# Shorter pauses between indirect transfers in a planned order, and a plan whose durations are read from a trace

## The chip, the cores and the metric

One core of a Trainium2 chip runs the whole kernel. The metric is the device time of one execution in microseconds, as the median of several runs. Five engines work beside each other, each on its own list of instructions in a fixed order: PE (matmuls), DVE (vector), ACT (activations and copies), POOL (here above all the issue of indirect transfers, and sums), and SP (the issue of plain transfers). Semaphores tie them together.

## What is computed

Pooled attention makes x, and a mixture of experts that takes the best expert for each token makes the output:

```python
q_pool = q.reshape(B, H, S // 2, 2, D).mean(axis=3)          # B=8, H=8, S=1152, D=64
scores = np.matmul(q_pool, k.transpose(0, 1, 3, 2)) / np.sqrt(D)
attn = softmax(scores)                                        # over the 1152 keys
x = np.matmul(attn, v).transpose(0, 2, 1, 3).reshape(4608, 512)

logits = x @ w_gate                                           # 8 experts
expert_idx = np.argmax(logits, axis=1)
for e in range(8):                                            # w1[e]: 512x1024, w2[e]: 1024x512
    xe = x[expert_idx == e]
    out[expert_idx == e] = gate_w[..., None] * (np.maximum(xe @ w1[e], 0) @ w2[e])
```

## The kernel before

**Attention** runs over 32 pairs (batch, two heads) and in each over two halves of the queries. A half has nine score products on PE (L543), each of which DVE takes out of PSUM (L548, `take`), an exponential on ACT in three pieces (L576), row sums folded on POOL (L622) and summed on PE (L631), and nine products with the values (L647). When the four pairs of a batch are done, the routing finds each token's expert, SP stores the rows of x to a table in DRAM (`x_runs`, L815), and POOL scatters each token's number and weight into its expert's list (`enlist`, L823, six indirect transfers per batch).

**The experts' stage** takes tokens in tiles. Two early tiles of 384 tokens, of the two experts with the most tokens so far, are cut while the last batch still runs. Then come the ranks: eight experts in the order of what is left to them, with tiles of (384, 288), (384, 256), (384, 224), (384, 192), (384, 160), (224, 192), (352) and (160) tokens. For a ranked tile POOL loads its piece of the list (`li`, L908), makes row numbers (`ix`, L918) and the tokens' numbers for the way back (`rec`, L921), and gathers 32 tokens at a time from `x_runs` (L924, `gather`): 12 gathers for 384 tokens. Buffers are `xr` (7) for the first and third 128 tokens of a tile and `xq` (4) for the second. DVE multiplies the rows with the token's weight (L1081, L1082, `weigh`) and transposes them (L1085); ACT casts them to the upper part `xh` (L1089), DVE makes the lower part `xl` (L1044). All products are made of such parts in three matmuls. PE makes the hidden layer (`ph`, L1138, 96 matmuls for a tile), ACT and DVE take it out (`hh` L1145, `hl` L1147), PE makes the output (`py`, L1167, 24 matmuls for every 128 tokens), ACT copies it (`y`, L1185, three buffers), and POOL scatters it to its tokens' places (L1175, `scatter`). The weights come by SP into six raw buffers and are split by ACT (`w1h`, `w2h`, L1106) and DVE (`w1l`, `w2l`, L1044); each part has one buffer, so that an expert's weights can be split only when the products of the one before have read theirs.

**The order** of all five engines is planned in the program, by `Flow`. Every step is added with its engine, a duration in ns, a key (its due place), what it waits for and the buffers that it holds. `emit` runs a model of the chip with these durations and gives each engine its list: whenever an engine is free in the model, it takes the ready step with the lowest key. Steps with the mark `paced` are the indirect transfers of POOL (L823, L924, L1175). Between the end of one in the model and the start of the next, CALM ns must pass. And the pause is made to hold on the chip too: when `trace` writes the instructions out, every paced transfer is tied by `in_step` to the last PE instruction written before it,

```python
if s[12] and self.pe is not None:
    self.pace(made, self.pe)      # a semaphore: no sooner than its place in the order
```

so that POOL, which could issue it when its data are there, waits until PE has ended that instruction. POOL works in order, and whatever stands behind the transfer on POOL waits too. The durations in the calls of `add` have no other use than this plan: no instruction depends on them except by its place.

## Time and profile before

| what | value |
|---|---|
| median of 3 runs | 1315.97 us (1315.13 to 1318.11) |
| profiled execution | 1319.63 us |
| its span | 1318.1 us |
| mean granted TensorE clock | 0.958 of full speed |
| PE busy | 1191.4 us, 90% |
| POOL busy | 878.7 us, 67% |
| DVE busy | 768.3 us, 58% |
| ACT busy | 628.4 us, 48% |

Busy shares are means over two stages: attention, up to about 745 us, and the experts' stage behind it. So the profile is read by stretches first, then by what PE waited for, and then along the engines that it waited for. The times in the rows are of the profiled execution and count from the start of its span. Idle time before an instruction is given with its releaser, the last thing that it waited for as far as semaphores show; "issue" means that nothing of that sort is seen.

### The profile page before, as it was taken

To read this page: it belongs to the slowest core of one execution; us is meant where nothing else is said; L and a number is where in the kernel's file an instruction comes from. 1 tells how busy PE (TensorE), PEld (TensorE's weight loads), DVE (VectorE), ACT (ScalarE), POOL (GpSimd) and SP (SyncE) were. 2 spreads that over 40 slices of the span, in tenths; PEclk is the share of its full clock that TensorE was granted. 3 is DMA by queue.
4 is the path that set the end of the run, shared out by engine and by line. 5 is a ranking of instruction groups with operands and counts; after the bars stand their busy time and mean duration, and the time that the engine had idled before them with its cause. 6 is when DMAs were issued, how large, how long until landed. Compare 5 with 4: busy or idle time off the path is not lost. (4 is left out here: it accounts for less than half of the span.)

```text
span 1318.1 us, 33770 instructions
## 1 busy us (share of the span) xinstructions
PE 1191.4 (90%) x14157; PEld 829.4 (63%) x14157; DVE 768.3 (58%) x2080; ACT 628.4 (48%) x768; POOL 878.7 (67%) x539
## 2 busy tenths in 40 slices
PE   7999999999999999999999897398996969699695
PEld 3555555555555555555555596297886868698695
DVE  5677768768677677687686584324443434334540
ACT  4657566565666666666664543212332222223340
POOL 2999899998999999999962523635454544434430
PEclk9999999999999999999999898799997979799898
DMA  6643334144243442352423256313323332324420
GB/s 181 151 122 86 108 98 145 48 110 130 73 113 106 112 115 82 104 140 63 115 64 115 87 143 187 102 29 99 108 88 110 94 113 75 120 67 139 157 76 19
DMA packets 76082, 138.12 MB, mean 105 GB/s; under 512 B 9859, under 2 KB 33311, under 8 KB 75920
## 3 DMA queue, kind: packets, MB, share of 16 engines
q1 hardware_dynamic: 65088, 116.18, 30.7%
q0 software_dynamic: 9744, 19.64, 5.3%
q8 instruction: 114, 1.87, 0.7%
q14 instruction: 48, 0.39, 0.1%
q10 hardware_dynamic: 1088, 0.03, 0.1%
HBM read 115.04 MB, written 21.02 MB: 103 GB/s over the span
## 5 line engine op out<-in xcount | busy, mean ns | idle before, releaser
L548 DVE TENSOR_SCALAR_CACHE_REDUCE s<-st 128x576 f32<-128x576 f32 x576 | 417.2, 753 | 166.9 <-PE st L543 166.0
L576 ACT ACTIVATE s<-s,bias 128x1728 f32<-128x1728 f32 x192 | 321.0, 1730 | 174.7 <-DVE bias L572 174.3
L543 PE MATMUL st<-qT,kT 64*64 64x288 f32 x4608 | 360.0, 411 | 18.6 <-DVE s L548 13.8
L647 PE MATMUL pa<-s,vn 64*64 64x288 f32 x4608 | 346.1, 405 | 0.2
L543 PEld LDWEIGHTS st<-qT,kT 64*64 64x64 f32 x4608 | 159.1, 133 | 164.5 <-DVE s L548 83.3
L622 POOL TENSOR_TENSOR fold<-s 128x1728 f32<-128x1728 f32 x58 | 224.3, 3868 | 14.4 <-ACT s L576 14.2
L1138 PE MATMUL ph<-xh,w1h 128*128 128x384 f32 (+6 forms) x512 | 165.6, 323 | 69.3 <-ACT xh L1089 68.3
L647 PEld LDWEIGHTS pa<-s,vn 64*64 64x64 f32 x4608 | 167.0, 133 | 93.3 <-DVE xT L653 6.7
L622 POOL TENSOR_TENSOR fold<-fold,s 128x1728 f32<-128x1728 f32 x58 | 224.5, 3871 | 1.0
L924 POOL DMA_INDIRECT xr<-x_runs,ix x104 | 118.1, 1136 | 131.6 <-PE ph L1138 43.6
L1138 PE MATMUL ph<-xl,w1h 128*128 128x384 f32 (+6 forms) x512 | 165.1, 322 | 1.0 <-DVE xl L1044 0.8
L1138 PE MATMUL ph<-xh,w1l 128*128 128x384 f32 (+6 forms) x512 | 163.6, 320 | 0.0
L1147 DVE SCALAR_TENSOR_TENSOR hl<-ph,hh 128x384 fp32r<-128x384 f32 (+5 forms) x100 | 55.0, 550 | 165.7 <-ACT hh L1145 154.1
L1138 PEld LDWEIGHTS ph<-xh,w1h 128*128 128x128 f32 x512 | 103.2, 202 | 73.7 <-ACT xh L1089 70.9
L1167 PE MATMUL py<-w2h,hh 128*128 128x512 f32 x328 | 128.7, 392 | 4.3 <-ACT y L1185 4.3
L1167 PE MATMUL py<-w2l,hh 128*128 128x512 f32 x328 | 128.5, 392 | 0.0
L1167 PE MATMUL py<-w2h,hl 128*128 128x512 f32 x328 | 128.3, 391 | 0.0
L1145 ACT ACTIVATE hh<-ph 128x384 fp32r<-128x384 f32 (+5 forms) x100 | 48.5, 487 | 159.6 <-PE ph L1138 157.8
L1175 POOL DMA_INDIRECT out_dram<-y,rec x41 | 44.8, 1092 | 113.0 <-issue 56.3
L1138 PEld LDWEIGHTS ph<-xl,w1h 128*128 128x128 f32 x512 | 102.8, 201 | 4.0 <-DVE xl L1044 3.5
L1138 PEld LDWEIGHTS ph<-xh,w1l 128*128 128x128 f32 x512 | 103.0, 201 | 0.0
L924 POOL DMA_INDIRECT xq<-x_runs,ix x44 | 52.7, 1197 | 62.0 <-PE py L1167 42.4
(176 smaller groups left out, 1313.5 us busy)
## 6 DMA issues: line engine op xcount, KB each, us to landing
raw<-in_moe_w_dram SPq DMA_DIRECT2D x80, 512.0 KB
qn<-in_q_dram SPq DMA_DIRECT2D x64, 384.0 KB
kn<-in_k_dram SPq DMA_DIRECT2D x32, 576.0 KB
vn<-in_v_dram SPq DMA_DIRECT2D x32, 576.0 KB
x_runs<-row SPq DMA_DIRECT2D x24, 396.0 KB
xr<-x_runs,ix POOLq DMA_INDIRECT x104
x_runs<-empty SPq DMA_DIRECT2D x4, 297.0 KB
lists<-re,di POOLq DMA_INDIRECT x48
```

What stands on the lines that cost most here:

```text
L543: made = nc.tensor.matmul(pt.t[to, h, :HQ], x.kT.t[up, c * P + i * D:c * P + (i + 1) * D], x.qT.t[up, cols], start=True, stop=True, tile_p ...
L548: nc.vector.tensor_scalar(s.t[:, c], pt.t[:, :, :HQ], -SCALE, None, op0=ALU.mult, op1=ALU.min, accum_out=mx.t[:, c:c + 1],)
L576: nc.scalar.activation(s.t[:, c0:c0 + n], s.t[:, c0:c0 + n], AF.Exp, bias=bias.t, scale=-1.0)
L622: add = lambda to, a, b: nc.gpsimd.tensor_tensor(to, a, b, ALU.add)
L647: made = nc.tensor.matmul(pa.t[cs, i, :HQ], x.vn.t[up, h, c, :], s.t[up, c, h], start=c == 0, stop=c == NC - 1, tile_position=(up.start, c ...
L924: return nc.gpsimd.indirect_dma_start(out=x.xr[i // NQD].t[:, i % NQD, :], out_offset=None, in_=xg, in_offset=bass.IndirectOffsetOnAxis(ap ...
L1138: made = nc.tensor.matmul(view()[:, i, :], a[:, c, fp], b[:, c, :n], start=c == 0 and k == 0, stop=c == NDC - 1 and k == 2)
L1145: a = f.add("ACT", act(nb * n) - 44, lambda fs=fs, view=view: nc.scalar.activation(hidden(m)[0][:, fs, :n], view(), AF.Relu), at - 20, don ...
L1147: d = f.add("DVE", dve(nb * n), lambda fs=fs, view=view: nc.vector.scalar_tensor_tensor(hidden(m)[1][:, fs, :n], view(), 0.0, hidden(m)[0] ...
L1167: made = nc.tensor.matmul(py.t, a[:, c, hs], b[:, c % 2, :], start=c == 0 and k == 0, stop=c == NFC - 1 and k == 2)
L1175: ins = nc.gpsimd.indirect_dma_start(out=out, out_offset=bass.IndirectOffsetOnAxis(ap=x.re.t[:up, r:r + 1], axis=0), in_=y.t[:up], in_offs ...
```

## The change

The pause gets two values, CALM 700 ns for the scatters into the lists and the gathers of early tiles, and CALM_X 500 ns for the gathers of ranked tiles and the scatters of outputs; `paced` is now that number. Beside this, durations in the plan are replaced: ACT's and POOL's base cost, the reductions, the exponential, PE's products and others. The core of the diff:

```diff
-CALM = 1300
+CALM, CALM_X = 700, 500
...
                 if s[12]:
-                    calm = free[e] + CALM
+                    calm = free[e] + s[12]
...
     def act(n):
-        return 110 + 0.833 * n
+        return 95 + 0.833 * n
...
     def pool(n):
-        return 185 + 2.137 * n
+        return 138 + 2.137 * n
...
-            m = f.add("PE", 460, product, at, done(*x.q[half], *x.k.get(c, ())), [pt, s, x.kT, x.qT], QUADS)
-            taken.append(f.add("DVE", 150 + dve(2 * HQ), take, at, done(m), [pt, s]))
+            m = f.add("PE", 452, product, at, done(*x.q[half], *x.k.get(c, ())), [pt, s, x.kT, x.qT], QUADS)
+            taken.append(f.add("DVE", dve(2 * HQ) + 20, take, at, done(m), [pt, s]))
...
-            e = f.add("ACT", act(2 * n * HQ) + 190, lambda c0=c0, n=n: expo(c0, n),
+            e = f.add("ACT", act(2 * n * HQ) + 95, lambda c0=c0, n=n: expo(c0, n),
...
-            outs.append(f.carry("POOL", 1230, lambda j=j: enlist(j), at + (K_PUT if b is None or b < B - 2 else 0) * j / NJ, done(p, *hold), [di, re], 40, paced=True))
+            outs.append(f.carry("POOL", 1230, lambda j=j: enlist(j), at + (K_PUT if b is None or b < B - 2 else 0) * j / NJ, done(p, *hold), [di, re], 40, paced=CALM))
...
-        x.rows = done(*(f.carry("POOL", 1310, lambda i=i: gather(i), key + i * 3 / x.nb, done(p, *stored), [x.ix, x.xr[i // NQD]], 400, paced=True)
+        x.rows = done(*(f.carry("POOL", 1310, lambda i=i: gather(i), key + i * 3 / x.nb, done(p, *stored), [x.ix, x.xr[i // NQD]], 400, paced=CALM if early else CALM_X)
...
-            p = f.add("DVE", dve(k * P) + 90, weigh, key + r, x.rows[r * NQD:r * NQD + k], [x.xr[r], x.li])
+            p = f.add("DVE", dve(k * P) + 180, weigh, key + r, x.rows[r * NQD:r * NQD + k], [x.xr[r], x.li])
...
-                    p = f.add("PE", 6 * n / 2.4 + 13, product, at,
+                    p = f.add("PE", 6 * max(n / 2.4 + 13, 110), product, at,
...
-                p = f.add("PE", 6 * DM / 2.4 + 14, product, at + c0, done(p, *x.w2_ready[c0 // 2], *x.made.get(c0, ()), *x.made.get(c0 + 1, ())),
+                p = f.add("PE", 6 * (DM / 2.4 + 13), product, at + c0, done(p, *x.w2_ready[c0 // 2], *x.made.get(c0, ()), *x.made.get(c0 + 1, ())),
...
-            a = f.add("ACT", act(DM) + 50, lambda y=y, py=py, up=up: nc.scalar.copy(y.t[:up], py.t[:up]),
+            a = f.add("ACT", act(DM) - 40, lambda y=y, py=py, up=up: nc.scalar.copy(y.t[:up], py.t[:up]),
                       at, done(p), [py, y])
-            f.carry("POOL", 1300, scatter, at, done(a), [y, x.re], 1200, paced=True)
+            f.carry("POOL", 1300, scatter, at, done(a), [y, x.re], 1200, paced=CALM_X)
```

Two places of the order. The first is POOL's list behind the last batch's scatters into the lists, where the first ranked tile is prepared. Before, with the second and the third scatter (L1175) of the first early tile's output, the loads of lists (li_10610 is that of the first ranked tile), its row numbers (ix_10693) and its first gather:

```order
L1175 DMA out_dram<-y_10511,rec_0_9583 4608x512
L884 TENSOR_LOAD ranked
L908 ISA
L908 DMA li_10653<-lists 128x1x18
L1175 DMA out_dram<-y_10569,rec_0_9583 4608x512
L918 TENSOR_SCALAR ix_10693<-li_10610,gid 128x12
L921 COPY rec_2_10695<-li_10610 32x3 x4
L884 TENSOR_LOAD ranked
L908 ISA
L908 DMA li_10710<-lists 128x1x24
L924 DMA xr_10721<-x_runs,ix_10693 128x132
```

After, from the load of the third ranked tile's list on (that of the first and second stand ahead of it; ix_10601 is now the first ranked tile's):

```order
L908 DMA li_10583<-lists 128x1x24
L918 TENSOR_SCALAR ix_10601<-li_10523,gid 128x12
L921 COPY rec_2_10603<-li_10523 32x3 x4
L884 TENSOR_LOAD ranked
L908 ISA
L908 DMA li_10618<-lists 128x1x16
L1175 DMA out_dram<-y_10621,rec_0_9635 4608x512
L918 TENSOR_SCALAR ix_10651<-li_10564,gid 128x9
L921 COPY rec_3_10653<-li_10564 32x3
L921 COPY rec_3_10653<-li_10564 32x2 x3
L924 DMA xr_10670<-x_runs,ix_10601 128x132
```

Two more loads of lists and the first ranked tile's row numbers have moved in front of the third scatter, and one load from behind its row numbers; the second tile's row numbers stand ahead of the first gather now.

The second place is POOL's list at the last gathers of the first tile of the third rank, of 384 tokens, the one whose first product is at 1000.43 in the trace. Its row numbers are ix_10860 before and ix_10801 after, and the outputs y_11796, y_11829, y_11869 before and y_11867, y_11906, y_11942 after are those of the first tile of the second rank. Before:

```order
L924 DMA xq_11965<-x_runs,ix_10860 128x132 x4
L924 DMA xr_12079<-x_runs,ix_10860 128x132 x4
L1175 DMA out_dram<-y_11796,rec_4_10790 4608x512
L1175 DMA out_dram<-y_11829,rec_4_10790 4608x512
L1175 DMA out_dram<-y_11869,rec_4_10790 4608x512
L1175 DMA out_dram<-y_12153,rec_5_10830 4608x512
L924 DMA xr_12196<-x_runs,ix_10883 128x132
```

After:

```order
L924 DMA xq_11735<-x_runs,ix_10801 128x132 x2
L924 DMA xr_11808<-x_runs,ix_10801 128x132 x4
L1175 DMA out_dram<-y_11867,rec_4_10687 4608x512
L924 DMA xr_11884<-x_runs,ix_10834 128x132 x2
L1175 DMA out_dram<-y_11906,rec_4_10687 4608x512
L924 DMA xr_11884<-x_runs,ix_10834 128x132 x2
L1175 DMA out_dram<-y_11942,rec_4_10687 4608x512
L924 DMA xq_11973<-x_runs,ix_10834 128x132 x3
```

Before, all three scatters of the earlier tile, and one of the tile behind it (y_12153), stand behind the last of the twelve gathers. After, the last gathers still stand ahead of these scatters, but the gathers of the next tile (ix_10834) are between the scatters too. A list of one engine does not show which PE instruction each transfer is tied to.

## Rows read from the trace of the kernel before

**Rows 1.** This is the table of stretches (from:to in us from the span's start). Columns: length of the stretch, then for each engine its busy time and in brackets its instructions, then TensorE's granted clock (1.00 is full speed), the DMA engines' mean busy share and GB/s:

```profile
25.00:385.00 360.00, 350.01 (x5753) 197.92 (x5746) 256.76 (x772) 231.30 (x244) 337.94 (x132) 1.00 0.39 106
385.00:745.00 360.00, 350.39 (x5706) 198.80 (x5701) 258.04 (x807) 215.40 (x239) 298.51 (x132) 1.00 0.35 99
...
1050.00:1100.00 50.00, 39.07 (x183) 34.95 (x182) 18.30 (x30) 12.09 (x20) 21.48 (x24) 0.86 0.32 103
...
1150.00:1200.00 50.00, 50.00 (x304) 45.28 (x304) 21.20 (x33) 16.68 (x26) 20.84 (x17) 1.00 0.35 106
```

**Rows 2.** This is the list of waits of PE between 740 and 1318 us. Columns: who waited for whom, then us in total, times, and the longest:

```profile
PE ph L1138 <- ACT xh L1089: 68.3, 7, 22.4
PE m L1026 <- DVE f L1025: 8.7, 1, 8.7
PE py L1167 <- ACT y L1185: 4.3, 1, 4.3
```

**Rows 3.** This is the timeline of PE, the rows that follow an idle time at the start of a tile's first product. Columns: start in us, us, engine, line, operation, out<-in, shape, and in brackets the idle time before it and what ended it:

```profile
856.99 0.69 PE L1138 MATMUL ph<-xh,w1h 128*128 128x384 f32 x1 [22.44 <-ACT xh L1089]
...
930.28 0.44 PE L1138 MATMUL ph<-xh,w1h 128*128 128x384 f32 x1 [1.66 <-ACT xh L1089]
...
1000.43 0.69 PE L1138 MATMUL ph<-xh,w1h 128*128 128x384 f32 x1 [11.00 <-ACT xh L1089]
...
1069.33 0.69 PE L1138 MATMUL ph<-xh,w1h 128*128 128x384 f32 x1 [10.89 <-ACT xh L1089]
...
1136.92 0.69 PE L1138 MATMUL ph<-xh,w1h 128*128 128x384 f32 x1 [9.91 <-ACT xh L1089]
...
1248.74 0.66 PE L1138 MATMUL ph<-xh,w1h 128*128 128x352 f32 x1 [10.61 <-ACT xh L1089]
```

**Rows 4.** This is the table of stretches again, with PE's half-clock stretches and one at full clock:

```profile
856.99:863.30 6.31, 6.27 (x18) 5.87 (x19) 1.23 (x2) 0.49 (x1) 1.06 (x1) 0.50 0.15 48
863.30:876.90 13.60, 13.60 (x80) 13.60 (x80) 4.09 (x8) 2.95 (x6) 6.17 (x10) 1.00 0.09 22
993.04:1006.70 13.66, 6.23 (x18) 5.84 (x19) 3.12 (x6) 2.07 (x4) 3.60 (x4) 0.50 0.40 144
1061.30:1074.96 13.66, 5.59 (x16) 5.19 (x17) 3.71 (x7) 2.02 (x4) 4.28 (x4) 0.50 0.45 164
1129.57:1143.20 13.63, 6.24 (x18) 5.84 (x19) 4.39 (x7) 2.16 (x4) 4.33 (x4) 0.50 0.58 183
1242.20:1252.45 10.25, 3.71 (x12) 3.40 (x13) 3.96 (x7) 1.61 (x3) 2.89 (x4) 0.50 0.39 147
931.60:935.00 3.40, 3.40 (x13) 3.40 (x12) 0.48 (x1) 0.39 (x1) 1.35 (x1) 0.50 0.86 266
921.36:924.80 3.44, 3.44 (x8) 2.69 (x9) 0.00 (x0) 0.59 (x1) 0.12 (x1) 0.50 0.09 20
```

**Rows 5.** This is the timeline of POOL, four gathers (L924): one beside a busy DVE, one that waits for nothing but the issue, the last of the tile whose first product is at 1000.43, and one in the middle of a tile:

```profile
752.04 3.47 POOL L924 DMA_INDIRECT xr<-x_runs,ix  x1 [0.30 <-issue]
...
850.62 1.00 POOL L924 DMA_INDIRECT xr<-x_runs,ix  x1 [0.30 <-issue]
...
992.37 1.25 POOL L924 DMA_INDIRECT xr<-x_runs,ix  x1 [0.30 <-issue]
...
1024.84 1.01 POOL L924 DMA_INDIRECT xq<-x_runs,ix  x1 [1.70 <-PE py L1167]
```

**Rows 6.** This is the timeline of DVE: two weight splits beside the gather of 752.04, the last split of w1 of an expert, and the weighing of the last gathered rows of the tile at 1000.43:

```profile
752.33 2.29 DVE L1044 TENSOR_TENSOR w1l<-raw,w1h 128x1024 fp32r<-128x1024 f32 x2
...
980.18 1.22 DVE L1044 TENSOR_TENSOR w1l<-raw,w1h 128x1024 fp32r<-128x1024 f32 x1
...
998.08 0.17 DVE L1081 TENSOR_TENSOR xr<-xr,li 128x16 f32<-128x16 f32 x1 [4.75 <-DMA xr<-x_runs,ix]
```

**Rows 7.** This is the timeline of POOL from the end of attention to the last gather of the first ranked tile: the load of that tile's list, the third scatter of the first early tile, the first gather, rec copies, gathers 4 and 5, gather 12:

```profile
798.88 0.79 POOL L908 DMA_DIRECT2D li<-lists  x1 [5.23 <-DMA lists<-re,di]
...
810.70 1.01 POOL L1175 DMA_INDIRECT out_dram<-y,rec  x1 [2.77 <-ACT hh L1145]
...
815.80 1.98 POOL L924 DMA_INDIRECT xr<-x_runs,ix  x1 [0.30 <-issue]
...
820.65 0.80 POOL L921 COPY rec<-li 32x2 int32<-32x2 int32 x3 [2.34 <-DMA xr<-x_runs,ix]
...
833.38 1.08 POOL L924 DMA_INDIRECT xr<-x_runs,ix  x1 [0.31 <-PE py L1167]
...
837.47 1.11 POOL L924 DMA_INDIRECT xq<-x_runs,ix  x1 [0.28 <-POOL rec L921]
...
851.93 1.00 POOL L924 DMA_INDIRECT xr<-x_runs,ix  x1 [0.30 <-issue]
```

**Rows 8.** This is the timeline of ACT: a cast of raw w2 and the third y copy of the first early tile:

```profile
798.03 1.04 ACT L1106 CAST w2h<-raw 128x1024 fp32r<-128x1024 f32 x1 [9.86 <-DMA raw<-in_moe_w_dram]
798.98 0.58 ACT L1185 COPY y<-py 128x512 f32<-128x512 f32 x1
```

**Rows 9.** This is the list of waits of PE between 25 and 745 us:

```profile
PE st L543 <- DVE s L548: 13.3, 40, 1.4
```

**Rows 10.** This is the groups of POOL's instructions by line and operation between 745 and 1318 us. Columns: line, engine, operation, out<-in, count, then busy us and mean ns of one, then idle time before them and its releasers:

```profile
L924 POOL DMA_INDIRECT xr<-x_runs,ix x87 | 100.2, 1152 | 92.8 <-PE ph L1138 43.6 <-PE py L1167 34.0 <-issue 8.7
L924 POOL DMA_INDIRECT xq<-x_runs,ix x44 | 52.7, 1197 | 62.0 <-PE py L1167 42.4 <-PE ph L1138 13.2 <-issue 4.8
```

More of the change, by code (lines that the diff above doesn't have):

```diff
@@ L97, in __init__, with add @@
         self.old, self.new, self.swap = set(old), set(new), swap
-    def add(self, eng, ns, fn, key=0.0, after=(), holds=(), tiled=False, late=0, paced=False):
+    def add(self, eng, ns, fn, key=0.0, after=(), holds=(), tiled=False, late=0, paced=0):
         if self.room is None:
@@ L110, in add, with carry @@
         return step
-    def carry(self, eng, ns, fn, key, after, holds, move, late=0, paced=False):
+    def carry(self, eng, ns, fn, key, after, holds, move, late=0, paced=0):
         s = self.add(eng, ns, fn, key, after, holds, paced=paced)
@@ L480, in load_pair @@
             done(q0), [qn, qp])
-        k1 = f.add("ACT", act(2 * NC * D) + 80, lambda: nc.scalar.copy(kp.t.rearrange("p c h d -> p h c d"), kn.t), key + K_POOL,
+        k1 = f.add("ACT", act(2 * NC * D), lambda: nc.scalar.copy(kp.t.rearrange("p c h d -> p h c d"), kn.t), key + K_POOL,
                    done(k0), [kn, kp])
@@ L510, in piece @@
             if ks:
-                e = f.add("ACT", act(nk * P), lambda: nc.scalar.copy(
+                e = f.add("ACT", act(nk * P) - 44, lambda: nc.scalar.copy(
                     kT.t[:, ks[0] * P:(ks[0] + nk) * P].rearrange("p (c r i) -> p r c i", r=2, i=D),
@@ L515, in piece @@
             if qs:
-                e = f.add("ACT", act(NQ), lambda: nc.scalar.copy(
+                e = f.add("ACT", act(NQ) - 44, lambda: nc.scalar.copy(
                     qT.t.rearrange("p (j r i) -> p r j i", r=2, i=QH),
@@ L567, in spread @@
                                      tile_position=(up.start, to.start))
-        m = f.add("DVE", 150, lambda: nc.vector.tensor_reduce(top.t, mx.t, axis=AX.X, op=ALU.min),
+        m = f.add("DVE", 110, lambda: nc.vector.tensor_reduce(top.t, mx.t, axis=AX.X, op=ALU.min),
                   key + 20 + K_MAX, done(*taken))
         m = f.add("PE", 130, spread, key + 20 + K_TOP, done(m), [pb], QUADS)
-        m = f.add("DVE", 290, lambda: nc.vector.tensor_reduce(bias.t, pb.t[:, :, :D], axis=AX.XY, op=ALU.min),
+        m = f.add("DVE", 250, lambda: nc.vector.tensor_reduce(bias.t, pb.t[:, :, :D], axis=AX.XY, op=ALU.min),
                   key + 20 + K_TOP, done(m), [pb])
@@ L649, in product @@
                 return made
-            p = f.add("PE", 460, product, key + 20.0 * c / NC, done(p, x.v, ready[c]), [pa, x.vn, s], QUADS)
+            p = f.add("PE", 452, product, key + 20.0 * c / NC, done(p, x.v, ready[c]), [pa, x.vn, s], QUADS)
         a = f.add("ACT", act(HQ) - 44, lambda: nc.scalar.copy(xT.t[:, hp, to], pa.t[:, 0, :HQ]), key + 20, done(p), [pa, xT])
-        return f.add("DVE", 100 + dve(HQ), lambda: nc.vector.tensor_tensor(
+        return f.add("DVE", dve(HQ), lambda: nc.vector.tensor_tensor(
             xT.t[:, hp, to], xT.t[:, hp, to], pa.t[:, 1, :HQ], ALU.add), key + 20, done(p, a), [pa, xT])
```

## The prediction

> **What bounds the kernel now.** I read the table of stretches first, and in it PE against the stretch's length. In attention (25 to 745 us) PE is busy 350 of 360 us in either half at the full clock [rows 1]: at most some 20 us can be had there, whoever causes them. After 745 us it is another kernel: 39.07 of 50 us busy at clock 0.86 in one stretch, 50.00 of 50 at 1.00 in another [rows 1], with the same work in both. So PE is the bound everywhere, and what can be won lies in the second stage, in holes that come and go.
>
> Next the list of waits: PE waits 68.3 us for ACT's casts of the gathered tokens (xh), in 7 times, of which one is 22.4 [rows 2]. PE's timeline shows where: 856.99 (22.44), 1000.43 (11.00), 1069.33 (10.89), 1136.92 (9.91), 1248.74 (10.61), each time the first product of a tile [rows 3]; beside them stand a wait of 8.7 for the flag and of 4.3 for a copy of y [rows 2]. The cast is not the cause, it is the last link of a chain; the links before it are on POOL. After a hole PE runs at half clock: 6.23 us of PE's time between 993.04 and 1006.70 stand at granted clock 0.50 (1.2 of 2.4 GHz), 18 matmuls of 0.35 us, where the same tile's form takes 13.60 / 80 = 0.17 at 1.00 [rows 4].
>
> Then POOL's timeline. A gather costs POOL 1.00 us and can start 0.30 after the one before (850.62, idle for the issue alone): a pitch of 1.30. In the middle of a tile they come at 2.7, like that of 1024.84, which takes 1.01 after 1.70 idle, and the releaser is PE [rows 5]. That is no shortage of data: PE's place in the order is the release, since every paced transfer waits for the PE instruction planned ahead of it, and the plan leaves 1300 ns between two. The tile of 1000.43 needs 12 gathers, and the last goes out at 992.37, when PE had ended its earlier work at 989.4; 5.7 us later DVE gets the rows (998.08, idle 4.75, releaser the gather), 2.35 later PE starts [rows 3, 5, 6]. The weights are not late: this expert's last w1l is split from 980.18 on, 1.22 us long, 8 us ahead of PE [rows 6].
>
> **The change part by part.** No instruction is added or taken out; what moves is the order, and with it the PE instruction that each paced transfer waits for.
>
> *Gathers and scatters of the ranked tiles.* The pause goes from 1300 to 500. I counted, in both programs, the matmuls that stand between the PE instruction that a gather waits for and its tile's first product. Before: for the 384-token tiles of the ranks after the first 186 to 24, 156 to 0, 162 to 0, 174 to 0, and 150 to 0 for the 352-token tile; the zeros are the last two or three gathers of the tiles that stall [rows 3]. After: 252 to 138, 312 to 192, 372 to 240, 480 to 312, 666 to 546. At 0.17 to 0.23 us a matmul, 138 are over 23 us ahead, against the 8.1 us from last gather to first product (992.37 to 1000.43). So the four holes from 1000.43 on [rows 3] go whole, and the 1.66 us at 930.28 too: 11.00 + 10.89 + 9.91 + 10.61 + 1.7 = 44.1. The scatters follow their y at once instead of behind a run of gathers, so that the 4.3 of the wait for y goes [rows 2], and a short wait behind it that I put at 1: 5.3. What is late next? By the same count the weights (8 us in hand) and DVE's own queue, which holds PE in no row of the undisturbed stretch 1150 to 1200 [rows 1].
>
> *The clock.* The half-clock stretches after these holes hold 6.23, 5.59, 6.24, 3.71, 3.40 and 3.44 us of PE's work [rows 4]; without the hole the same work takes half: 14.3 us. I take all of it, since between 1150 and 1200, where no tile waits, the granted clock stays 1.00 [rows 1].
>
> *The first ranked tile (22.44).* Here data are late. The lists have landed at 798.88 before (idle 5.23, releaser the lists); index and first gather wait until 815.80 because the third scatter of the early tile is put ahead of them (810.70); gathers 1 to 12 then take 36.1 us, for index steps of the next five tiles with loads stand between them, whose rec copies wait for the gather before to land (2.34 at 820.65) [rows 7]. After: the six scatters into the lists stand 31 PE instructions earlier (some 6 us at 0.2) with five pauses that are each 0.6 shorter (3 us), so the lists are there at about 790; loads and the first index stand ahead of the third scatter, and that waits only for its y, copied at 798.98 + 0.58 behind the cast that waits for raw weights [rows 8]. Third scatter, index step and gather 1: about 804.6 (802.5 if the place in the order lets it, 808 if the index step waits for a landing). Gathers 1 to 12 with four index steps between, of 4.1 (833.38 to 837.47) to 4.5 us, two loads (2.4) and five pitches of 1.3: 18 + 4.8 + 6.5 = 29.3. Gather 12 at 833.9, product 5.1 later (851.93 to 856.99) at 839.0, where PE is free at 834.55 [rows 3, 7]. Hole 4.4 instead of 22.44: 18.0; half of its half-clock time, 6.27 / 4 = 1.6 [rows 4]. Together 19.6, with bounds 14 and 24.
>
> *The flag's 8.73* stays: behind it stands a cast of raw weights that landed late (798.03, idle 9.86 for the load) [rows 8], and the same cast holds the relu copies behind it on ACT. Bounds: nothing, or 4 us.
>
> *The durations.* They change no instruction, only the plan of attention. It has 20 us of idle PE in all [rows 1], 13.3 of it in 40 waits for DVE's reduction of scores [rows 9]. By the two programs PE changes between its tiling modes 235 times, from 207; no row prices a change, the plan's own number is 0.15 us (SWITCH), so 28 x 0.15 = 4 us, with bounds of -6 (a better order takes a third of the idle 20) and +9 (twice that price). Weighing on DVE, which is in order, now stands earlier and may hold a relu copy in the first ranked tiles: 2 us, bounds 0 and 6.
>
> Sum: 44.1 + 5.3 + 14.3 + 19.6 - 4 - 2 = 77.3. The profiled execution takes 1319.63 us, 3.66 over the median of the runs; 1319.63 - 77.3 = 1242.3, and 1315.97 - 77.3 = 1238.7 for the median.
>
> What POOL pays: 131 gathers after 745 us take 1.15 and 1.20 us on the mean [rows 10], but one takes 3.47 (752.04) [rows 5], beside two w1l splits that DVE begins at 752.33 [rows 6], each with two inputs in SBUF. So a gather can be held by DVE, and closer gathers meet it no less. At the means POOL is busy some 21 of 50 us and has room [rows 1]. The Trainium skill (SBUF — State Buffer, "SBUF: two separate sides") states that a transfer issued by GpSimd is held for the whole length of a DVE operation that takes the port pair they share, and gives 620 against 3100 ns. By that rule as a general one, rival 4 below would hold; the one long row agrees with it, the means do not.
>
> **The rivals.** 1. *The first ranked tile does not shrink*: the index steps still wait for landings, the lists land late because rows and weights share the queues. For it: 2.34 and 5.23 of idle time are landings [rows 7]. Price 19.6: 1258.
> 2. *Gathers stand early but their buffers come late*: a gather must also wait for DVE to have read the buffer of an older tile (7 and 4 buffers). If half of the 44.1 + 5.3 + 14.3 us of the later tiles stays: 1271. Against it: the order places them where a model with these buffers has them free.
> 3. *Slower: attention loses its slack.* The planned DVE take of a score chunk falls from 817 to 687 ns, and there are two score buffers. If the plan is now tighter than the engine, each of 576 score products waits for DVE. The 40 waits now average 0.33 us [rows 9]; at 0.2 us for each product 576 x 0.2 = 115: 1238.7 + 115 = 1354. It turns the sign from 77 / 576 = 0.13 us on. Against it: DVE is busy 257 of 360 us there and catches up [rows 1].
> 4. *Gathers are slow, not early*: if most met a DVE operation and took 3.47 like that of 752.04, 131 x 3.77 = 494 us of POOL, and 41 scatters of 1.35 us pitch more, 549 in the 573 us of the stage: POOL would bind, and the time stay near 1316.
> 5. *The pause is not the cause*: the holes come from something else that the order does not touch, and the time stays 1316. Against it: zeros in the count stand exactly at the tiles with holes.
>
> **How the numbers follow.** The forecast has 0.74, rival 1 0.10, rival 2 0.08, rival 3 0.04, rivals 4 and 5 0.02 each. The forecast's own bounds: the first tile 5 either way, attention 10 and 5 about its 4, the flag 4, DVE 4: which seldom fall together: some 14 either way. The range goes from 1224 to rival 1 with its own spread, 1262; it leaves out rivals 2 to 5 (0.16) and little of the forecast. 0.2%, 2.6 us, is about what a measurement can tell from no change. Faster: forecast, rivals 1 and 2, 0.92; same: 4 and 5, 0.04; slower: 3, 0.04.
>
> **What would show it.** Right: PE's waits for xh fall from 68.3 to under 10 us, all in the first ranked tile, and the half-clock stretches after 900 us are gone; POOL's gathers come 1.3 to 2 us apart and land tens of us before DVE weighs them. The first ranked tile's product starts near 839. Attention ends within 5 us of where it did. Wrong: a hole before a tile's first product with DVE idle for a gather's landing (rivals 1, 2), gathers of 3 us in rows (4), or waits of scores for DVE in the hundreds (3).

## The result, and the profile after

| | before | after |
|---|---|---|
| median | 1317.04 us (4 runs, 1315.13 to 1320.14) | 1253.72 us (4 runs, 1251.86 to 1255.77) |
| ratio | | 0.9517, 95% interval 0.9491 to 0.9544 |
| profiled execution | 1319.63 us | 1251.86 us |
| mean granted clock | 0.958 | 0.982 |

63 us less by the medians, 68 by the two profiled executions; 77 was forecast. The time lies in the range, and the holes went where the forecast had them; the sum was 10 to 14 us too high.

The table of stretches of the kernel after, with the same columns as before:

```profile
25.00:385.00 360.00, 349.78 (x5722) 198.80 (x5726) 258.45 (x772) 232.30 (x243) 331.11 (x129) 1.00 0.39 104
...
745.00:800.00 55.00, 50.01 (x333) 40.65 (x326) 44.83 (x107) 29.02 (x52) 24.13 (x21) 0.94 0.57 162
800.00:850.00 50.00, 35.60 (x158) 30.72 (x157) 21.29 (x32) 14.60 (x22) 34.67 (x55) 0.87 0.49 153
...
900.00:950.00 50.00, 49.22 (x257) 44.03 (x256) 19.35 (x31) 14.26 (x23) 30.78 (x37) 1.00 0.34 104
950.00:1000.00 50.00, 46.65 (x257) 42.17 (x256) 26.49 (x42) 17.39 (x28) 34.97 (x36) 1.00 0.43 132
...
1100.00:1150.00 50.00, 50.00 (x319) 45.28 (x319) 19.94 (x29) 16.79 (x26) 8.48 (x8) 1.00 0.35 112
```

Where rows 1 had 39.07 of 50 us at clock 0.86, PE is now busy 46.7 to 50 of 50 at 1.00 from 900 us to 1200. What is left stands between 745 and 850 us, and in short waits behind that. PE's list of waits from 740 us on:

```profile
PE ph L1138 <- ACT xh L1089: 8.6, 2, 6.0
PE ph L1138 <- DVE hl L1147: 8.5, 7, 2.6
PE py L1167 <- DVE hl L1147: 6.1, 1, 6.1
PE ph L1138 <- DVE xl L1044: 2.1, 2, 1.5
```

The 68.3 us for xh are 8.6, the waits for the flag and for y are gone [rows 2], and another releaser has come up: hl, DVE's half of the hidden layer, 14.6 us, which had 1.0 before. PE's timeline shows the places:

```profile
825.72 0.79 PE L1167 MATMUL py<-w2h,hl 128*128 128x512 f32 x1 [6.10 <-DVE hl L1147]
...
845.26 0.69 PE L1138 MATMUL ph<-xh,w1h 128*128 128x384 f32 x1 [5.95 <-ACT xh L1089]
...
975.19 0.45 PE L1138 MATMUL ph<-xh,w1h 128*128 128x384 f32 x1 [2.63 <-DVE hl L1147]
...
1035.66 0.44 PE L1138 MATMUL ph<-xh,w1h 128*128 128x384 f32 x1 [2.42 <-DVE hl L1147]
```

845.26 is the first product of the first ranked tile, 11.7 us earlier than in rows 3 and with 5.95 instead of 22.44 us of hole. The four holes of 10 us have no counterpart. POOL's timeline, with the list of the first ranked tile, its row numbers, the third scatter of the first early tile, copies of the second tile's `rec`, the first and the last gather of the first ranked tile, and the last two gathers of the 384-token tile of the third rank (at 992.37 in rows 5):

```profile
796.76 0.79 POOL L908 DMA_DIRECT2D li<-lists  x1 [5.08 <-DMA lists<-re,di]
...
802.48 1.25 POOL L918 TENSOR_SCALAR ix<-li,gid 128x12 int32<-128x12 int32 x1 [2.12 <-DMA li<-lists]
...
806.34 1.09 POOL L1175 DMA_INDIRECT out_dram<-y,rec  x1 [0.31 <-PE ph L1138]
...
810.01 0.62 POOL L921 COPY rec<-li 32x2 int32<-32x2 int32 x3 [1.11 <-DMA out_dram<-y,rec]
811.08 1.16 POOL L924 DMA_INDIRECT xr<-x_runs,ix  x1 [0.45 <-POOL rec L921]
...
838.76 1.34 POOL L924 DMA_INDIRECT xr<-x_runs,ix  x1 [0.30 <-issue]
...
933.98 1.00 POOL L924 DMA_INDIRECT xr<-x_runs,ix  x1 [0.36 <-PE py L1167]
935.34 1.00 POOL L924 DMA_INDIRECT xr<-x_runs,ix  x1 [0.36 <-PE py L1167]
```

The first product of that tile of the third rank now starts at 968.20: the last gather goes out 33 us ahead of it, where it was 8.1. And DVE's timeline ahead of the wait at 975.19:

```profile
970.36 0.18 DVE L1081 TENSOR_TENSOR xr<-xr,li 128x16 f32<-128x16 f32 x1 [3.72 <-DMA xr<-x_runs,ix]
970.57 0.69 DVE L1082 TENSOR_TENSOR xr<-xr 128x512 f32<-128x512 f32 x1
971.18 3.49 DVE L1044 TENSOR_TENSOR w2l<-raw,w2h 128x1024 fp32r<-128x1024 f32 x3
974.58 1.01 DVE L1147 SCALAR_TENSOR_TENSOR hl<-ph,hh 128x384 fp32r<-128x384 f32 x2
```

A weighing (L1081) of a later tile stands at the head of DVE's list and waits 3.72 us for its gather; three splits of w2 and then hl, for which PE waits, stand behind it. The wait of 6.10 at 825.72, in the second early tile, is made in the same way, by a weighing of the first ranked tile's rows:

```profile
823.58 0.18 DVE L1081 TENSOR_TENSOR xr<-xr,li 128x16 f32<-128x16 f32 x1 [10.11 <-DMA xr<-x_runs,ix]
...
825.15 0.52 DVE L1147 SCALAR_TENSOR_TENSOR hl<-ph,hh 128x384 fp32r<-128x384 f32 x1
```

The gathers have not become longer: POOL's groups from 745 us on, columns as in rows 10:

```profile
L924 POOL DMA_INDIRECT xr<-x_runs,ix x90 | 98.7, 1097 | 50.9 <-PE ph L1138 20.4 <-issue 14.3 <-PE py L1167 10.1
L924 POOL DMA_INDIRECT xq<-x_runs,ix x44 | 51.3, 1167 | 20.1 <-PE ph L1138 6.9 <-issue 6.1 <-PE py L1167 6.0
```

### The profile page after: what moved, and what is told of

Same layout as the page of the kernel before. It is cut to its first block, busy times and chain, and to the rows that moved or that the text cites. A ratio compares the mean times of both kernels' runs of the same rounds, so it can differ in the third digit from the quotient of the medians.

```text
span 1250.3 us, 33779 instructions
## 1 busy us (share of the span) xinstructions
PE 1178.0 (94%) x14157; PEld 817.4 (65%) x14157; DVE 769.7 (62%) x2080; ACT 628.7 (50%) x768; POOL 874.2 (70%) x539
## 4 chain that ended last, share of the span: by engine, by line
PE 67%; POOL 10%; DVE 8%; issue 8%; DMA 5%; ACT 1%; POOLq 0%; SPq 0%; DVEq 0%; ACTq 0%
PE st L543 17%; PE pa L647 16%; PE py L1167 14%; PE ph L1138 12%; POOL fold L622 7%; DVE s L548 4%; PE sums L631 2%; PE st L499 2%; DMA xq<-x_runs,ix 1%; DMA xr<-x_runs,ix 1%; PE sums L617 1%; POOL lists L823 1%; DMA raw<-in_moe_w_dram 1%; PE st L505 1%; POOL out_dram L1175 1%
## 5 line engine op out<-in xcount | busy, mean ns | idle before, releaser
L1138 PE MATMUL ph<-xh,w1h 128*128 128x384 f32 (+6 forms) x512 | 159.2, 311 | 17.3 <-ACT xh L1089 8.6
L924 POOL DMA_INDIRECT xr<-x_runs,ix x104 | 112.8, 1085 | 80.7 <-PE ph L1138 20.4
L1138 PE MATMUL ph<-xl,w1h 128*128 128x384 f32 (+6 forms) x512 | 157.9, 308 | 2.1 <-DVE xl L1044 2.1
L1138 PE MATMUL ph<-xh,w1l 128*128 128x384 f32 (+6 forms) x512 | 157.5, 308 | 0.0
L1175 POOL DMA_INDIRECT out_dram<-y,rec x41 | 48.6, 1185 | 137.6 <-PE py L1167 81.6
L1138 PEld LDWEIGHTS ph<-xh,w1h 128*128 128x128 f32 x512 | 97.8, 191 | 22.2 <-DVE hl L1147 11.8
L1138 PEld LDWEIGHTS ph<-xl,w1h 128*128 128x128 f32 x512 | 97.9, 191 | 3.5 <-DVE xl L1044 2.9
L1138 PEld LDWEIGHTS ph<-xh,w1l 128*128 128x128 f32 x512 | 97.9, 191 | 0.0
L823 POOL DMA_INDIRECT lists<-re,di x48 | 45.9, 956 | 67.7 <-PE st L543 27.3
```

The lines of the kernel that those rows point to most:

```text
L823: ins = nc.gpsimd.indirect_dma_start(out=lists, out_offset=bass.IndirectOffsetOnAxis(ap=di.t[:, j:j + 1], axis=0), in_=re.t[:, j, :], in_o ...
L924: return nc.gpsimd.indirect_dma_start(out=x.xr[i // NQD].t[:, i % NQD, :], out_offset=None, in_=xg, in_offset=bass.IndirectOffsetOnAxis(ap ...
L1138: made = nc.tensor.matmul(view()[:, i, :], a[:, c, fp], b[:, c, :n], start=c == 0 and k == 0, stop=c == NDC - 1 and k == 2)
L1175: ins = nc.gpsimd.indirect_dma_start(out=out, out_offset=bass.IndirectOffsetOnAxis(ap=x.re.t[:up, r:r + 1], axis=0), in_=y.t[:up], in_offs ...
```

## The experiments

Each was run beside the kernel before on the same chip, four times or more. Three chips were used, on which the kernel before took 1317.4, 1317.6 and 1317.4 us, so that medians from different chips can be set side by side. Ratios are to the kernel before. The mark "..." stands for lines left out.

**The pauses alone.** The kernel before with the three pauses and no other number:

```diff
-CALM = 1300
+CALM, CALM_X = 700, 500
...
-                    calm = free[e] + CALM
+                    calm = free[e] + s[12]
```

> The kernel before with the three pauses alone (700 and 500 ns), all durations of the plan as before. Theory (the pause, made a wait by its place in the order, is what the holes come from, and the new durations cost some 6 us in attention): the holes before 1000.43 and later go and attention keeps its old end near 745, so 1244 to 1252 us. Rival (the new durations, not the pauses, carry a good part of the gain, by bringing steps into another order): 1270 or more. A second rival (the 6 us of attention come from where the paced transfers now stand, not from the durations): 1252 to 1258.

Measured: 1249.84 us, ratio 0.9496 (0.9467 to 0.9526). The pauses carry the whole gain. Attention's last product starts at 744.9 in its trace, 745.2 before, 751.2 after. What is left of PE's waits, from its timeline, for comparison with the runs that follow:

```profile
799.50 0.69 PE L1138 MATMUL ph<-xh,w1h 128*128 128x384 f32 x1 [5.69 <-DVE hl L1147]
...
841.25 0.69 PE L1138 MATMUL ph<-xh,w1h 128*128 128x384 f32 x1 [8.08 <-ACT xh L1089]
...
967.96 0.45 PE L1138 MATMUL ph<-xh,w1h 128*128 128x384 f32 x1 [1.94 <-DVE hl L1147]
...
1028.71 0.69 PE L1138 MATMUL ph<-xh,w1h 128*128 128x384 f32 x1 [4.25 <-DVE hl L1147]
```

The hole of 8.08 stands before the first ranked tile. The wait of 5.69 is behind a weight split on DVE, the other two for hl behind a weighing that waits for its gather.

**The durations alone.** The kernel after with all pauses at 1300 ns:

```diff
-CALM, CALM_X = 700, 500
+CALM, CALM_X = 1300, 1300
```

> The kernel after with all pauses set back to 1300 ns, so only the durations of the plan are new. Theory: the holes of about 10 us before the first product of a tile stay, and attention is 6 us longer: 1315 to 1325 us. Rival (the durations carry a good part of the gain): under 1295.

Measured: 1311.49 us, ratio 0.9952 (0.9936 to 0.9969): neither 1315 to 1325 nor the rival's, but near no change. PE's waits from 740 us on:

```profile
PE ph L1138 <- ACT xh L1089: 52.1, 6, 23.1
PE ph L1138 <- DVE hl L1147: 16.7, 2, 13.2
```

Holes for xh are shorter by 16 us and waits for hl longer by as much (13.2 of these at 814.22, behind raw weights that landed late: ACT is idle 13.93 us for them before its cast at 811.39). Of the waits for the flag (8.7) and for y (4.3) in rows 2 only 0.3 for y is left. The holes before later tiles stay, but not all at 10 us: 7.56, 10.40, 6.86 and 2.52. The new durations are worth 6 us under the old pauses and nothing under the new ones.

**No tie, the order as it was.** The kernel before, with the waits of ranked gathers and scatters for a PE instruction left out:

```diff
-                if s[12] and self.pe is not None:
+                if s[12] == 1 and self.pe is not None:
...
-        x.rows = done(*(f.carry("POOL", 1310, lambda i=i: gather(i), key + i * 3 / x.nb, done(p, *stored), [x.ix, x.xr[i // NQD]], 400, paced=True)
+        x.rows = done(*(f.carry("POOL", 1310, lambda i=i: gather(i), key + i * 3 / x.nb, done(p, *stored), [x.ix, x.xr[i // NQD]], 400, paced=1 if early else 2)
...
-            f.carry("POOL", 1300, scatter, at, done(a), [y, x.re], 1200, paced=True)
+            f.carry("POOL", 1300, scatter, at, done(a), [y, x.re], 1200, paced=2)
```

> The kernel before, its order unchanged on every engine, but the gathers of ranked tiles and the scatters of outputs are no longer tied to a PE instruction; the transfers of attention and the early tiles still are. Theory (the tie to PE's place is what makes the gathers late): the four holes of 10 us after 1000 go without any move of an instruction, POOL's gathers come at a pitch near 1.3 us, and the time falls by 45 to 65, to 1252 to 1272; the first ranked tile keeps most of its 22 us. Rival (buffers, the landing of data or POOL's own speed make the gathers late): 1300 or more. The run may also show a cost that the tie prevents: gathers that collide with other transfers or wait for a buffer at the head of POOL's list, with scatters and PE's y copies behind them.

Measured: 1286.94 us, ratio 0.9774 (0.9744 to 0.9804), between theory and rival: 30 of the 68 us that the pauses give come with the tie alone. The holes are 5.5 to 7.2 us now, where they were 9.9 to 11.0. For the 384-token tile of the third rank, POOL's, ACT's, DVE's and PE's timelines show why (956.01 is its last gather, and 978.70 DVE's weighing of its last rows):

```profile
956.01 1.01 POOL L924 DMA_INDIRECT xr<-x_runs,ix  x1 [0.30 <-issue]
...
970.83 1.05 ACT L1106 CAST w2h<-raw 128x1024 fp32r<-128x1024 f32 x1 [4.71 <-PE py L1167]
...
971.91 2.59 DVE L1044 TENSOR_TENSOR w2l<-raw,w2h 128x1024 fp32r<-128x1024 f32 x2 [4.45 <-ACT w2h L1106]
...
978.70 0.17 DVE L1081 TENSOR_TENSOR xr<-xr,li 128x16 f32<-128x16 f32 x1
...
981.03 0.69 PE L1138 MATMUL ph<-xh,w1h 128*128 128x384 f32 x1 [6.17 <-ACT xh L1089]
```

All gathers are out by 957, 24 us ahead of the product, and still their rows are weighed at 978.70 only. The weighing stands in DVE's list behind the splits of w2, and these wait for ACT's casts (4.45), which wait for the products of the expert before (4.71). So a hole of before had two halves: gathers that went out late, and lists of DVE and ACT that were made for late gathers. The plan's pause set both: with shorter pauses both go, without the tie only the first.

**Attention's durations as before.** The kernel after, with ten of its numbers set back:

```diff
-            m = f.add("PE", 452, product, at, done(*x.q[half], *x.k.get(c, ())), [pt, s, x.kT, x.qT], QUADS)
-            taken.append(f.add("DVE", dve(2 * HQ) + 20, take, at, done(m), [pt, s]))
+            m = f.add("PE", 460, product, at, done(*x.q[half], *x.k.get(c, ())), [pt, s, x.kT, x.qT], QUADS)
+            taken.append(f.add("DVE", 150 + dve(2 * HQ), take, at, done(m), [pt, s]))
...
```

> The kernel after, but with the ten durations of attention's steps (copies, score and value products, reductions, exponential) as before; pauses and durations of the experts' stage as after. Theory (the 6 us that attention lost come from these durations): attention ends near 745 and the time is 1246 to 1250 us, some 5 below after. Rival (they come from the places of the paced transfers, or from the base costs of ACT and POOL): attention ends near 751, 1252 to 1256.

Measured: 1250.41 us, ratio 0.9494 (0.9467 to 0.9521), attention's last product at 745.5. The place moved as the theory had it; the interval overlaps that of after (0.9491 to 0.9544), so that the 3 us between them are not shown by the times.

**The pauses, with attention's new durations.** The other way round: those ten numbers of after in the run with the pauses alone.

```diff
-            m = f.add("PE", 460, product, at, done(*x.q[half], *x.k.get(c, ())), [pt, s, x.kT, x.qT], QUADS)
-            taken.append(f.add("DVE", 150 + dve(2 * HQ), take, at, done(m), [pt, s]))
+            m = f.add("PE", 452, product, at, done(*x.q[half], *x.k.get(c, ())), [pt, s, x.kT, x.qT], QUADS)
+            taken.append(f.add("DVE", dve(2 * HQ) + 20, take, at, done(m), [pt, s]))
...
```

> The run with the three pauses alone (1249.8 us, attention ends at 744.9), with the ten new durations of attention's steps and all others as before. Theory (these durations lengthen attention by some 5 us): attention ends between 748 and 752 and the time is 1252 to 1256 us. Rival (attention's 6 us in the run of after are a change from execution to execution, or come from the base costs of ACT and POOL): attention ends below 747 and the time is 1247 to 1251 us.

Measured: 1273.19 us, ratio 0.9675 (0.9658 to 0.9692): the sign of the theory and some four times its size, 23 us above the run with the pauses alone. Attention's last product is at 761.8, 17 us later, and 14.79 us of hole stand before the first ranked tile, where that run has 8.08. PE's waits in attention:

```profile
PE st L543 <- DVE s L548: 9.6, 34, 0.5
PE sums L631 <- POOL fold L622: 6.1, 2, 5.9
```

One wait of 5.9 us for POOL's fold, and TensorE's granted clock, account for part of the 17 us: the clock is 0.83 between 240 and 260 us, behind that wait (it ends at 254.43), and 0.91 between 600 and 620, where the run with the pauses alone has 1.00 from 20 us to the end of attention. By PE's work at half clock (5.0 and 3.5 us) this makes some 4 us, an estimate. The rest is spread, and its cause stays open. The wait of scores for DVE is no longer than in rows 9. That this set of durations gives a longer attention is shown; which of the ten does it, and why it is less in the kernel after, whose other durations are new too, is not. Nor is it shown that each of the ten is nearer to the trace; DVE's take is: two in a row start 0.67 us apart in the trace of before (309.82 and 310.49), and the plan has 0.687 now and had 0.817.

**The lists' pause back at 1300.** The run with the pauses alone, with

```diff
-CALM, CALM_X = 700, 500
+CALM, CALM_X = 1300, 500
```

> The run with the three pauses alone, but 1300 ns again for the scatters into the lists and the early gathers; 500 ns for ranked gathers and scatters of outputs. Theory (nearly all of the gain is in the ranked tiles, the shorter pause of the lists moved their landing by 2 us only): 1249 to 1255 us. Rival (the earlier lists carry the 18 us of the first ranked tile, as the prediction put part of it): 1258 to 1268 us.

Measured: 1264.28 us, ratio 0.9593 (0.9571 to 0.9616): the rival. POOL's timeline (the first list, first gather) and PE's first ranked product:

```profile
799.64 0.79 POOL L908 DMA_DIRECT2D li<-lists  x1 [6.83 <-DMA lists<-re,di]
...
814.76 1.88 POOL L924 DMA_INDIRECT xr<-x_runs,ix  x1 [0.30 <-issue]
...
854.62 0.69 PE L1138 MATMUL ph<-xh,w1h 128*128 128x384 f32 x1 [21.22 <-ACT xh L1089]
```

The first tile's hole is back at 21.22 us. The same rows in the run with the pauses alone are a list at 791.75, a first gather at 807.01 and a hole of 8.08: the pause of 700 ns carries 14 us, and 13.4 of them are there at the first ranked tile's first product (841.25 there, 854.62 here).

**Row numbers later.** The run with the pauses alone, where the index step of a ranked tile is planned behind the landed gathers of the tile before:

```diff
-        p = f.add("DVE" if early else "POOL", 650, index, key - LEAD, done(p), [x.li, x.ix, x.re])
+        p = f.add("DVE" if early else "POOL", 650, index, key - LEAD, done(p, *([] if early else behind)), [x.li, x.ix, x.re])
...
+        if not early:
+            behind[:] = x.rows
         return x
```

> The run with the three pauses alone, where the row numbers of a ranked tile are planned behind the landing of the gathers of the ranked tile before it, so that no index step stands between the twelve gathers of the first ranked tile. Theory (these steps, whose rec copies wait for the gather before to land, make the first ranked tile late): its gathers come 1.3 to 1.9 us apart, the hole of 8.1 us before its first product goes, with its half-clock time: 1238 to 1243 us. Rival (its data are late for another reason, such as the lists or the landing of the gathers): the hole stays above 4 us, 1246 to 1252 us.

Measured: 1234.79 us, ratio 0.9377 (0.9358 to 0.9396): the theory, with 3 us more than its range had. POOL's timeline, first and last gather of the first ranked tile, and PE's first product of it (two lines were added, so L1138 is L1140 here):

```profile
804.36 1.08 POOL L924 DMA_INDIRECT xr<-x_runs,ix  x1 [0.30 <-issue]
...
826.75 1.20 POOL L924 DMA_INDIRECT xr<-x_runs,ix  x1 [0.36 <-PE py L1169]
...
834.86 0.44 PE L1140 MATMUL ph<-xh,w1h 128*128 128x384 f32 x1 [2.94 <-ACT xh L1091]
```

The twelve gathers take 22.4 us instead of 27.4, and start 2.7 earlier; the hole is 2.94 instead of 8.08, and this product starts 6.4 us earlier. The edit did more than the theory had: from this product to PE's last one the trace is 7.1 us shorter too (384.4 against 391.4), with the later waits of 1.94 and 4.25 gone and one of 2.74 in their place. So no more than about half of the 15 us is the first ranked tile's.

**Landing planned later.** The run with the pauses alone, where the plan takes a ranked gather to land 2500 ns later:

```diff
-        x.rows = done(*(f.carry("POOL", 1310, lambda i=i: gather(i), key + i * 3 / x.nb, done(p, *stored), [x.ix, x.xr[i // NQD]], 400, paced=CALM if early else CALM_X)
+        x.rows = done(*(f.carry("POOL", 1310, lambda i=i: gather(i), key + i * 3 / x.nb, done(p, *stored), [x.ix, x.xr[i // NQD]], 400, late=0 if early else 2500, paced=CALM if early else CALM_X)
```

> The run with the three pauses alone, where the plan takes the landing of a ranked gather 2.5 us later, so that the weighing of its rows stands later in DVE's list. Theory (PE's waits for hl at a tile of each rank come from a weighing that was planned ahead of hl and waits for its gather): the waits of 1.94 and 4.25 us go, and some at the end of the first ranked tile grow or stay: 1243 to 1248 us. Rival (hl waits for something else, as the weight splits on DVE): no change, 1248 to 1252 us.

Measured: 1239.14 us, ratio 0.9406 (0.939 to 0.9422): the theory, with more than it expected. PE's waits from 745 us on:

```profile
PE ph L1138 <- ACT xh L1089: 13.3, 2, 11.6
PE ph L1138 <- DVE hl L1147: 6.0, 1, 6.0
```

In the run with the pauses alone they are 9.8 for xh and 11.9 for hl in three waits. The waits of 1.94 and 4.25 at later tiles are gone; one of 6.0 at 799.64 stays as it was (5.69), and the first ranked tile's hole has grown to 11.6. From the first ranked tile's first product to PE's last one the trace is 10.9 us shorter; 6.2 of it are those two waits, and most of the rest is the clock. The table of stretches of the run with the pauses alone, columns as in rows 1, directly behind the two:

```profile
967.96:974.00 6.04, 6.04 (x26) 6.04 (x27) 0.97 (x2) 0.49 (x1) 1.41 (x2) 0.72 0.58 202
1028.71:1035.00 6.29, 6.29 (x23) 6.29 (x24) 0.96 (x2) 0.49 (x1) 1.35 (x2) 0.60 0.54 188
```

With a later landing the clock is 1.00 from 849.50 us to PE's last product.

**The short pauses without the tie.** The run with the pauses alone, its order unchanged, the tie kept only where the mark is CALM (lists and early gathers):

```diff
-                if s[12] and self.pe is not None:
+                if s[12] == CALM and self.pe is not None:
```

> The run with the three pauses alone (1249.8 us), its order unchanged, with the ranked gathers and the scatters no longer tied to PE. Theory: with the short pauses the tie no longer holds gathers that matter (POOL issues them 0.30 us apart while DVE waits), so 1246 to 1251 us. Rival (the waits of 1.94 and 4.25 us for hl, behind a weighing that waits for its gather, come from the tie): these waits go, 1240 to 1245 us.

Measured: 1238.72 us, ratio 0.9401 (0.9385 to 0.9416): the rival, and a little more. The waits for hl at later tiles are gone here too, so that they can be mended from either side: gathers that go out when POOL can, or weighings planned for when gathers land.

**No pause.** The run with the pauses alone, with CALM_X 0, which leaves out the tie too:

```diff
-CALM, CALM_X = 700, 500
+CALM, CALM_X = 700, 0
```

> The run with the three pauses alone, with 0 ns for ranked gathers and scatters: no pause in the plan and no tie. Theory (below 500 ns POOL's own work sets the pace, a gather takes 1.0 to 1.3 us plus 0.30, so the plan is then ahead of POOL): like the run without the tie at 1238.7, or some us more where the plan weighs rows before they land: 1237 to 1248 us. Rival (without a pause the gathers crowd out other transfers, and row stores or weights come late): 1250 or more.

Measured: 1252.88 us, ratio 0.9521 (0.95 to 0.9541), 14 us more than the same without the tie at 500 ns, and above what theory had. The time is the rival's, but not by its mechanism: a gather lands 2.6 (`xr`) and 2.9 us (`xq`) after its issue on the median, against 2.6 and 2.7 in the run without the tie. PE's waits:

```profile
PE ph L1138 <- DVE hl L1147: 27.2, 6, 8.1
PE ph L1138 <- ACT xh L1089: 1.7, 1, 1.7
```

The last of the waits for hl ends at 1037.15, 4.19 us long. DVE's timeline ahead of it:

```profile
1035.93 0.23 DVE L1081 TENSOR_TENSOR xq<-xq,li 128x8 f32<-128x8 f32 x1 [5.90 <-DMA xq<-x_runs,ix]
1036.20 0.43 DVE L1082 TENSOR_TENSOR xq<-xq 128x256 f32<-128x256 f32 x1
1036.55 0.55 DVE L1147 SCALAR_TENSOR_TENSOR hl<-ph,hh 128x384 fp32r<-128x384 f32 x1
```

27.2 us for hl, 1.7 for xh. 6.5 of the 27.2, at 801.45, stand behind a weight split, as in the run with the pauses alone; the other five stand behind a weighing that was idle before it, four of the five for a gather, one (5.21 at 970.68) for something that the semaphores do not name. A plan that lets POOL gather faster than it can puts the weighings so early in DVE's list that they wait there, with hl behind them.

**Both edits, and both without the tie.** The two single edits on top of the pauses:

```diff
-        p = f.add("DVE" if early else "POOL", 650, index, key - LEAD, done(p), [x.li, x.ix, x.re])
+        p = f.add("DVE" if early else "POOL", 650, index, key - LEAD, done(p, *([] if early else behind)), [x.li, x.ix, x.re])
...
+        if not early:
+            behind[:] = x.rows
...
-                        [x.ix, x.xr[i // NQD]], 400, paced=CALM if early else CALM_X)
+                        [x.ix, x.xr[i // NQD]], 400, late=0 if early else 2500, paced=CALM if early else CALM_X)
```

> The two single edits on top of the three pauses together: row numbers of a ranked tile planned behind the gathers of the tile before (1234.8 us alone), and the landing of ranked gathers planned 2.5 us later (1239.1 alone). Theory (they mend different places: the hole before the first ranked tile, and hl behind a weighing at later tiles): what is left of hl waits at later tiles goes, 1229 to 1233 us. Rival (both mend the same waits): 1234 to 1237.

Measured: 1232.98 us, ratio 0.9364 (0.9348 to 0.938). That is in the theory's range, but its interval overlaps that of the run with later row numbers (0.9358 to 0.9396), so the 2 us between them are not shown by the times. By the trace, of the waits for hl one of 5.5 us near 803 is left and 0.7 in two others.

And on top of that:

```diff
-                if s[12] and self.pe is not None:
+                if s[12] == CALM and self.pe is not None:
```

> As the run with both edits, with the ranked gathers and scatters no longer tied to PE. If the tie is only a cost once the plan is right, 1 to 4 us less than that run; if it no longer matters, the same within 2 us; if untied transfers collide with rows, weights or lists at the end of attention, 2 to 5 us more.

Measured: 1232.08 us, ratio 0.936 (0.9345 to 0.9376): the same within 2. With a plan that is right about landing the tie costs nothing that can be measured. These two are the fastest kernels here, 21 to 22 us below after.

## Why the prediction was right, and where its sum was off

**The range.** The median, 1253.72, is 15 us above the forecast's 1238.7 and 1 us outside the forecast's own bounds, 14 either way. The stated range holds it because it was drawn up to rival 1, whose 1258 is the nearer number. But rival 1 did not happen: the first ranked tile's hole fell from 22.44 to 5.95. So the sign, the places and the main cause were right, and that the range holds the number is in part luck. Of the signs that were named, xh fell under 10 us (2.7 of it at an early tile) and the half clock behind 900 us is gone. Attention ended 6 us later, where 5 was the limit. And one sign failed: gathers do not land long before DVE weighs their rows. DVE's weighings wait 73.5 us for gathers behind 745 us, and waited 72.1 before.

**The later tiles.** The four holes went whole, as forecast, and the clock stays at 1.00 behind them. From the first ranked tile's first product to PE's last one the traces have 1303.85 - 856.99 = 446.9 us before and 1236.43 - 845.26 = 391.2 after: 55.7 less. The terms for holes, y and clock made 63.7, and the first ranked tile's half-clock time, 1.6, falls here too: 65.3. Of the shortfall of 9.6, waits for hl make 7.7 (six, from 859.96 on) and one for xl at 847.45 makes 1.5. The term that was mis-sized is what DVE's list costs PE, the answer to "what is late next?". It stood at nothing for the later tiles, because the stretch 1150 to 1200 had no such wait, and at 2 us, bounds 0 and 6, for the first ranked tiles. All waits for hl in the kernel after make 14.6 us, 1.0 before. The cause of those at later tiles is the weighing at the head of DVE's list: in the run with the pauses alone a later landing and the missing tie each took the like waits at later tiles away, and DVE's rows of the kernel after have the same form.

**The tie.** The prediction called PE's place in the order the release of the gathers. That was half of it: the run without the tie gave 30 us, and by its rows DVE's and ACT's lists had been made for late gathers too. The forecast held because a shorter pause in the plan moves both.

**The first ranked tile.** From the second early tile's first product (789.59 and 796.40) to this tile's the time fell from 67.4 to 48.9 us: 18.5 less, where 18.0 of the term belongs here. 16.5 of it is the hole. All times here are 6.8 us later than in the forecast, which left attention where it was; counted from the second early tile's first product, the first gather stands at 14.7 us (forecast 15.0) and the tile's product at 48.9 (forecast 49.4). But the links between are not the forecast's. The third scatter did not go out with its y, which ACT had copied by 798.41; it came at 806.34, behind the first index step, which waited for its list (802.48). And the next index step's copies waited for that scatter to land (810.01), which the forecast had as a bound only. The gathers took 27.7 us, forecast 29.3. So the mechanism is right, earlier lists and a shorter run of gathers, and that the first gather's place came out so closely is in part luck. That the lists' earlier places carry this term is shown by the run with 1300 ns for them (14 us), and that index steps between the gathers hold a part of what is left by the run that moved them (the hole 2.94 instead of 8.08).

**The flag's 8.73** was forecast to stay and went: the raw weights whose late load stood behind it are waited for 1.92 us now, where it was 9.86 [rows 8]. ACT's timeline:

```profile
796.87 1.05 ACT L1106 CAST w2h<-raw 128x1024 fp32r<-128x1024 f32 x1 [1.92 <-DMA raw<-in_moe_w_dram]
```

Why they are at hand sooner is not shown. In the run with the pauses alone ACT still waits 7.00 us for them (795.01), and PE 5.69 at 799.50. In the kernel after there is instead the wait of 6.10 at 825.72, in the second early tile, behind a weighing of the first ranked tile's rows that waits 10.11 us for its gather. The two nearly cancel.

**Attention** was given 4 us more, with bounds of -6 and +9: 6.0 by the two traces. Its cause is shown in part only. In the eleven traces with the old durations attention's last product starts between 744.7 and 749.0, and executions of one planned order differ by up to 4.1 (the pauses alone, with the tie and without it). In the three with the new durations it starts at 748.3 (the durations alone), 751.2 (after) and 761.8 (the pauses with attention's new durations). So that the durations can lengthen attention is shown by the last; how much of the 6.0 in the one trace of the kernel after is theirs is not. The price by changes of tiling mode is not shown. Scores waiting for DVE (rival 3) did not grow: 11.8 us in 34 waits after, 13.3 in 40 before [rows 9].

**Gathers beside DVE** (rival 4): the means fell from 1.15 and 1.20 to 1.10 and 1.17 us while gathers came closer. The Trainium skill (SBUF — State Buffer, "SBUF: two separate sides") states that a transfer that GpSimd issues is held for the whole length of a DVE operation that takes the port pair they share; that fits single rows like that of 752.04 [rows 5], and no mean here shows it.

The three stretches add up: 55.7 + 18.5 - 6.8 = 67.4, against 67.8 between the two spans; the 6.8 are attention's 6.0 and 0.8 from its end to the second early tile's first product.

## What to carry to other kernels

A pause in a plan that becomes a semaphore on the chip is paid twice: the transfer goes out late, and every engine's list behind it is made for the late arrival. Taking the wait away gives back the first half only; the plan must know when data land. And it must not be too bold: with planned pauses of 0 instead of 500 ns, both without the tie, the kernel lost 14 us, since work waits at the head of an in-order list, and what stands behind it, here hl, stops the engine that is the bound. When a hole is to go, read on the engine in front of the bound what stands in its list behind the next wait; that is where the remainder shows up.

## What the runs showed of the hardware that was not expected

POOL issues twelve gathers in a row at a pitch of 1.30 us (the run without a pause, 917.18 to 931.50). From issue to landing a gather takes 2.6 to 2.9 us on the median and 7.0 at worst, in six traces with short pauses or none, with and without the tie. Where the plan was right about landing, gathers cost PE nothing that can be measured with or without the tie.

The granted clock also falls without a long hole: in attention of the kernel after it is 0.91 between 320 and 340 us, where PE had waited 0.38, 0.22, 0.71 and 0.72 us between 317.6 and 321.5. In the run with the pauses alone the 6 us behind a wait of 1.94 us have 0.72.

Attention in the same planned order ended between 744.9 and 749.0 us in two traces, about the spread that the runs of one kernel show (2 to 5 us in most). A plan with other durations of the same steps made it 17 us longer in one run.
